# Earlier load requests, and a last weight chunk in two column halves, in an attention and soft-MoE kernel

## The chip, the cores and the metric

The kernel runs on one core of one Trainium2 chip. The metric is the device time in microseconds of one execution, the median of several runs. The profile is one profiled execution on the chip, with a time of its own. Engines: PE is the matrix engine TensorE (PEld is its weight load), DVE is VectorE, ACT is ScalarE, POOL is GpSimd and SP is SyncE, which here only issues transfers. Each engine works through its own program in order. Transfers run on 16 DMA engines that all queues share.

## What is computed

The reference is attention with 16 extra "beacon" keys and values ahead of the sequence, and a soft mixture of experts on its output:

```python
# q, k, v: (8 batches, 8 heads, 576, 64); beacon_k, beacon_v: (8, 8, 16, 64), float32
k_all, v_all = concat([beacon_k, k], 2), concat([beacon_v, v], 2)
scores = q @ k_all^T / 8                # causal over the 576, the beacons always seen
x = softmax(scores) @ v_all             # as 4608 tokens x 512
# phi: (512, 32 slots), w1: (8 experts, 512, 1024), w2: (8, 1024, 512)
logits = x @ phi
d = softmax(logits, axis=0)             # over the tokens
slot_input = (d.T @ x).reshape(8, 4, 512)
slot_out[e] = relu(slot_input[e] @ w1[e]) @ w2[e]
out = softmax(logits, axis=1) @ slot_out
```

No output row can be formed before the last expert's weights have been used, since each output token mixes all 32 slots.

## The kernel before

**The order of the work.** The order on every engine is the order of the program's text; there is no scheduler that moves work. Buffers come from pools that rotate: a load into a buffer waits until the last reader of its earlier content is done, and it is issued at its place in the program of its engine, so whatever stands behind it on that engine waits too.

**Attention** runs over 32 pairs of heads, n = 0 to 31; batch b = n // 4, and g = n % 4 is the pair within the batch. Iteration n (L758 to L797) issues the scores of pair n (`scores`, four banks; ScalarE takes the exponential, L526, and GpSimd masks it, `select`, L512), the transposes of the keys (even n) or queries (odd n) of the next half batch (`transposes`, L490), and the product of pair n-1's masked scores with the values (`attend`, L542). So `attend(4)` stands in iteration 5. At g = 1, 2 and 3 the values of the next batch are cast (`cast_v`, L391 and L395), and at g = 3 they are permuted (`perm_v`). In `perm_v` GpSimd copies the 16 beacon values into place (L410), in order with its masks. Iterations 0 and 1 are written out ahead of the loop, with all loads that fit at the start.

**Loads.** k and q come by half batches (a half batch is four heads, numbered m = 2b + hb here) through four buffers each; v and its remainder `vrem` by batches through two buffers each; the beacon values `bvst` through one buffer. All of them are issued by SyncE (only the first q by ScalarE). At g = 0 of batch b SyncE's program has the beacon values of batch b + 1, then v of b + 2, then k and q of its first half; at g = 2 the remainder of v and the second half.

**Weights.** The 16.8 MB of expert weights, as float16, come in 32 chunks of 512 KB (`wchunks`). GpSimd issues them, since they are cast on the way from float32. `load_weights(count)` at the end of an iteration issues the next `count` of them. Experts 0 to 4 have memory of their own (expert 4 among them with both matrices); expert 5 uses the two v buffers (`wv`), experts 6 and 7 the k and q buffers (`wt`), once attention is done with them. The last chunk, `WLAST`, is half of the second matrix of expert 7; it comes as two transfers, each of two of its four row groups c.

**The end.** `first` and `second` are the two expert matrices, for four experts at a time in the four column groups of TensorE. `second(eg, c0, c1, halves)` adds the row groups c0 to c1 into the left (256 columns) and right accumulators. The left half is scaled into `so1` by VectorE (L873), the right by ScalarE (L876). Then every token's output is one matmul with `so1` (L924), scaled on the way out of PSUM by VectorE (L931) or ScalarE (L929) in turn, and stored three token columns j at a time (L935), 768 KB each; the first three columns are stored as one and two.

```python
        second(1, 0, NFC - 2)
        second(1, NFC - 2, NFC, (0,))
        nc.vector.tensor_scalar(out=so1[:, 0:HW], in0=so[0], scalar1=rd[:, 0:1], scalar2=None,
                                op0=AL.mult)
        second(1, NFC - 2, NFC, (1,))
        nc.scalar.activation(so1[:, HW:Dm], so[1], AF.Copy, scale=rd[:, 0:1])
```

Behind it stands a test of value ranges (`judge`) and a general path that is entered only if the test fails.

Of the kernel before, what the change touches and what calls it, by code (L numbers as in the profile page):

```python
# [9 lines left out]
FP = mybir.dt.float32  # L10
# [3 lines left out]
AL = mybir.AluOpType  # L14
AF = mybir.ActivationFunctionType
# [36 lines left out]
NJ = 9  # L52
# [216 lines left out]
def kernel(  # L269
# [12 lines left out]
    nc = tc.nc  # L282
    P = 128
    B, H, S, D = q.shape
    Nb = beacon_k.shape[2]
    E, Dm, F = moe_w1.shape
# [3 lines left out]
    NFC = F // P  # L290
# [4 lines left out]
    scale = 1.0 / (D ** 0.5)  # L295
# [45 lines left out]
        g = n % NG  # L341
        return 2 * g + hh if n >= NPAIR - 2 else 4 * (g // 2) + 2 * hh + g % 2

    def load_qk(b, hb, first=False):
        for src, tag in ((k, "k"), (q, "q")):
            t = st[tag, b, hb] = stq.tile([P, 2, NJ, D], FP, name=f"{tag}stag", tag=tag)
            sr = src[b].rearrange("h (p j) d -> (h p) (j d)", j=NJ)
            eng = nc.scalar if first and tag == "q" else nc.sync
            for h0, h1 in ((0, 1), (1, 2)) if first else ((0, 2),):
                lo = 256 * hb + P * h0  # L350
                eng.dma_start(
                    out=t[:, h0:h1, :, :].rearrange("p h j d -> p h (j d)"),
                    in_=sr[lo:lo + P * (h1 - h0), :].rearrange("(h p) e -> p h e", p=P))

    def load_v(b):

        t = st["v", b] = stv.tile([P, H, 4, D], FP, name="vstag", tag="v", bufs=2)
        st["r", b] = stv.tile([P, H, D], FP, name="vrem", tag="r", bufs=2)
        h0 = 0 if b else 1
        lo = ((b * H + h0) * S - Nb) * D
        nc.sync.dma_start(
            out=t[:, h0:H, :, :].rearrange("p h t d -> p h (t d)"),
            in_=v.rearrange("b h s d -> (b h s d)")[lo:lo + (H - h0) * S * D].rearrange(
                "(h e) -> h e", h=H - h0)[:, 0:4 * P * D].rearrange("h (p e) -> p h e", p=P))
        if b == 0:
            nc.vector.memset(t[0:4, 0, :, :], 0.0)  # L370
            for p0, p1 in ((4, 116), (116, 128)):
                nc.sync.dma_start(
                    out=t[p0:p1, 0, :, :].rearrange("p t d -> p (t d)"),
                    in_=v[b, 0, 4 * p0 - Nb:4 * p1 - Nb, :].rearrange("(p t) d -> p (t d)", t=4))

    def load_vr(b):
        nc.sync.dma_start(out=st["r", b][0:80, :, :],
                          in_=v[b, :, 496:576, :].rearrange("h p d -> p h d"))

    def load_bv(b):  # L380

        st["bv", b] = stv.tile([Nb, H, D], FP, name="bvst", tag="bv", bufs=1)
        nc.sync.dma_start(out=st["bv", b][:, :, :], in_=beacon_v[b].rearrange("h n d -> n h d"))
# [39 lines left out]
    def piece(e, m, j):  # L423

        if e < NRES:
            if m == 0:
                return w1h[e][:, 2 * j:2 * j + 2, :].rearrange("p t f -> p (t f)")
            return w2h[e][:, 4 * j:4 * j + 4, :].rearrange("p c d -> p (c d)")
        if (e, m, j) not in wtail:
            if e == NRES:  # L430
                t = stv.tile([P, 2, 2048], F16, name="wv", tag="v", bufs=2)
                for i in range(2):
                    wtail[e, m, i] = t[:, i, :]
            else:
# [10 lines left out]
    def load_weights(count):  # L445
        for _ in range(count):
            if not wchunks:
                return
            e, m, j = wchunks.pop(0)
            if m == 0:  # L450
                nc.gpsimd.dma_start(
                    out=piece(e, m, j),
                    in_=moe_w1[e, 2 * j * P:2 * (j + 1) * P, :].rearrange("(p t) f -> p (t f)", t=2))
            else:
                src = moe_w2[e].rearrange("(p c) d -> p c d", c=NFC)
                cs = 2 if (e, m, j) == WLAST else 4
                for c in range(0, 4, cs):
                    nc.gpsimd.dma_start(
                        out=piece(e, m, j)[:, c * Dm:(c + cs) * Dm],
                        in_=src[:, 4 * j + c:4 * j + c + cs, :].rearrange("p c d -> p (c d)"))  # L460

    qTs = {}

# [213 lines left out]
    with tc.manual_schedule(engines={ET.PE, ET.DVE, ET.Activation, ET.Pool, ET.SP}):  # L677
# [11 lines left out]
        load_vr(1)  # L689
        phif = acc[:, 0:NDC * NSL].rearrange("p (c e) -> p c e", c=NDC)  # L690
        nc.sync.dma_start(out=phif, in_=moe_phi.rearrange("(c p) e -> p c e", p=P))
        load_bv(1)

        nc.gpsimd.memset(eT[:, 0:512], 1.0)
        nc.gpsimd.memset(onesh[:, :], 1.0)  # L695
# [57 lines left out]
        transposes(1, 1)  # L753
        scores(1, 3)
        load_v(2)
        load_qk(2, 0)

        for n in range(2, NPAIR):  # L758
            b, g = divmod(n, NG)
            scores(n, 0)  # L760
            scores(n, 1)
            if n == 2:
                cast_v(1, 0)
            if n // 2 + 1 < 2 * B:
# [12 lines left out]
            if b and g == 2:  # L777
                logits(b - 1)
            if n >= 8 and g == 0:
                dispatch(b - 2)  # L780
            if b + 1 < B and g:
                if b or g > 1:
                    cast_v(b + 1, g - 1)
                if g == 3:
                    perm_v(b + 1)
            if b + 1 < B and g == 0:
                load_bv(b + 1)
            if b + 2 < B:
                if g == 0:
                    load_v(b + 2)  # L790
                    load_qk(b + 2, 0)
                if g == 2:
                    load_vr(b + 2)
                    load_qk(b + 2, 1)
            if n == 5:
                nc.vector.tensor_copy(out=phih[:, :, :], in_=phif)
            load_weights(0 if b == 0 else (0, 1, 1, 1)[g] if b < 6 else (1, 2, 2, 2)[g] if b == 6 else 2)  # L797
        siz = work.tile([P, NDC, E * (NSL + SPE)], F16, name="siz", tag="qT")
        nc.gpsimd.memset(siz[:, :, :], 0.0)
        load_weights(len(wchunks))  # L800
# [79 lines left out]
        ps_f = fast.enter_context(tc.tile_pool(name="ps_f", bufs=6, space=PSUM))  # L880
        outr = out.rearrange("(a p j) d -> a p j d", p=P, j=NJ)


        gd = fast.enter_context(tc.tile_pool(name="gdp", bufs=1))
# [29 lines left out]
        JS = [(0, 3), (3, 6), (6, 9)]  # L914
        cnt = 0
        for bb in range(4):
            for (j0, j1) in JS if bb else [(0, 1), (1, 3)] + JS[1:]:
                osb = m3.tile([P, 3, Dm], FP, name="osb", tag="osb")
                for j in range(j0, j1):
                    hw = Dm // 2 if cnt == 0 else Dm  # L920
                    fp_ = [ps_f.tile([P, Dm], FP, name="fps", tag="fps")
                           for _ in range(Dm // hw)]
                    for i, f in enumerate(fp_):
                        nc.tensor.matmul(f[:, 0:hw], row_tokens(bb, j),  # L924
                                         so1[:, hw * i:hw * i + hw], start=True, stop=True)
                    for i, f in enumerate(fp_):
                        ou = osb[:, j - j0, hw * i:hw * i + hw]
                        if (cnt + i) % 2:
                            nc.scalar.activation(ou, f[:, 0:hw], AF.Copy, scale=rc[:, bb, j:j + 1])  # L929
                        else:  # L930
                            nc.vector.tensor_scalar(out=ou, in0=f[:, 0:hw],  # L931
                                                    scalar1=rc[:, bb, j:j + 1], scalar2=None,
                                                    op0=AL.mult)
# [41 lines left out]
```

## Time and profile before

| what | value |
|---|---|
| median of 3 runs | 201.09 us (200.14 to 202.2) |
| the profiled execution | 200.37 us |
| its span, first to last instruction | 198.7 us |
| PE busy | 160.2 us (81%) |
| DVE, ACT, POOL busy | 135.1, 133.9, 118.6 us |
| read from memory, written to it | 62.71 MB, 9.44 MB |
| loads of SyncE and stores | 25,736 packets, 38.01 MB, 53.4% of 16 engines' span |
| weights (GpSimd's queue) | 4,752 packets, 16.78 MB, 43.2% |

A line of a timeline gives the start in us from the span's start, the length, the engine, the program line, the operation, what it writes and reads, and how many were merged; in brackets stands the idle time of the engine before it and what ended it. In a table by stretch, each engine's busy time is followed by its number of instructions; then come the granted TensorE clock (1.00 is full), the mean busy share of the DMA engines, and GB/s. The bytes of the weights are counted as they arrive (float16), so that weights alone read some 213 GB/s with all engines full. The DMA share can pass 1, because the packets of one DMA engine overlap a little. The records behind the page also hold the landings of each transfer (one on each of the DMA engines that take part) and the start, length and size of each packet.

### The profile page before, as it was taken

The numbers are of one execution on the slowest core, as the hardware profiler recorded it, in microseconds if no ns is written. First come the engines' busy times: TensorE is split into PE (matmuls) and PEld (weight loads), VectorE is DVE, ScalarE is ACT, GpSimd is POOL, SyncE is SP. The second block draws the span as 40 slices with busy tenths as digits, with TensorE's granted clock in tenths as the row PEclk, the third lists the DMA queues.
The fourth block names the chain that finished last, engine by engine and source line by source line (L and its number), as shares of the span: only waits on it lengthen the run. The fifth ranks groups of instructions, "written<-read, shape, count | busy, mean of one in ns | idle before, by whom it ended". The sixth has DMA issues, their size and how long they took to land.

```text
span 198.7 us, 7454 instructions
## 1 busy us (share of the span) xinstructions
PE 160.2 (81%) x3160; PEld 107.9 (54%) x3160; DVE 135.1 (68%) x282; ACT 133.9 (67%) x173; POOL 118.6 (60%) x270
## 2 busy tenths in 40 slices
PE   6978697898998989889898998988899944984400
PEld 2525455675774867567586576756676622541000
DVE  1497778888878887878898888888373300797400
ACT  3285678888887898888888889888942200892400
POOL 6074396697596678759758877997873000781000
PEclk9999999999999999999999999999999995897555
DMA  6999998999999999999999999999999994399992
GB/s 214 352 380 406 355 365 261 366 332 179 237 386 277 235 373 315 258 305 366 259 255 366 290 273 199 188 178 215 214 210 214 212 213 91 153 426 428 416 417 80
DMA packets 30817, 55.93 MB, mean 282 GB/s; under 512 B 8380, under 2 KB 16568, under 8 KB 30776
## 3 DMA queue, kind: packets, MB, share of 16 engines
q1 hardware_dynamic: 25736, 38.01, 53.4%
q0 software_dynamic: 4752, 16.78, 43.2%
q8 instruction: 26, 0.43, 0.8%
q10 hardware_dynamic: 288, 0.59, 0.8%
q14 instruction: 15, 0.12, 0.2%
HBM read 62.71 MB, written 9.44 MB: 363 GB/s over the span
## 4 chain that ended last, share of the span: by engine, by line
PE 55%; DMA 16%; ACT 8%; DVE 7%; POOL 5%; issue 3%; ACTq 0%; DVEq 0%; POOLq 0%
DMA wt<-in_moe_w_dram 14%; PE av L542 13%; PE sc L521 13%; PE trps L490 8%; PE fps L924 5%; PE xtps L568 5%; ACT vh L408 4%; ACT expT L526 3%; PE vpt L405 2%; POOL expT L512 2%; PE vps L405 2%; DMA bkf<-in_beacon_k_dram 2%; PE lgps L587 2%; PE sips L626 2%; DVE sel L729 2%
## 5 line engine op out<-in xcount | busy, mean ns | idle before, releaser
L526 ACT ACTIVATE expT<-sc 128x992 f16<-128x992 f32 (+3 forms) x128 | 104.3, 868 | 17.6 <-PE sc L521 16.8
L512 POOL TENSOR_SCALAR_AFFINE_SELECT expT<-expT 128x224 f16<-128x224 f16 (+3 forms) x128 | 55.2, 442 | 28.2 <-ACT expT L526 27.0
L521 PE MATMUL sc<-qT,kT 64*128 64x80 bf16 (+4 forms) x576 | 43.0, 244 | 12.1 <-ACT expT L526 5.7
L542 PE MATMUL av<-vh,expT 128*128 128x65 f16 (+1 forms) x960 | 40.3, 194 | 0.4 <-issue 0.2
L542 PEld LDWEIGHTS <-expT 128*128 128x128 f16 (+1 forms) x960 | 33.5, 98 | 4.1 <-issue 1.0
L521 PEld LDWEIGHTS <-kT 64*128 64x128 bf16 x576 | 17.1, 95 | 28.6 <-issue 21.4
L502 DVE COPY kT<-trps 128x640 bf16<-128x640 bf16 (+1 forms) x31 | 22.7, 773 | 8.9 <-PE trps L490 8.4
L502 DVE COPY qT<-trps 128x640 bf16<-128x640 bf16 (+1 forms) x31 | 22.7, 772 | 8.0 <-PE trps L490 6.9
L556 DVE TENSOR_TENSOR x<-av,r 128x640 f16<-128x640 f32 x32 | 26.4, 824 | 1.1
L391 POOL CAST vc<-vstag 128x512 f16<-128x512 f32 x30 | 17.5, 613 | 3.3 <-PE sc L521 3.3
L575 DVE COPY xT<-xtps 128x576 f16<-128x576 f16 x31 | 14.2, 457 | 4.3 <-PE xtps L568 4.3
L929 ACT ACTIVATE osb<-fps,rc 128x512 f32<-128x512 f32 (+1 forms) x19 | 11.9, 675 | 5.0 <-PE fps L924 4.5
L931 DVE TENSOR_SCALAR osb<-fps,rc 128x512 f32<-128x512 f32 (+1 forms) x18 | 12.2, 724 | 2.5 <-PE fps L924 2.3
L568 PE MATMUL xtps<-idh,x 128*128 128x128 f16 (+2 forms) x160 | 13.7, 216 | 0.1
L924 PE MATMUL fps<-so,eT 128*128 128x512 f16 (+1 forms) x37 | 12.0, 456 | 0.4 <-ACT osb L929 0.2
L893 POOL TENSOR_SCALAR lo<-so 128x512 f32<-128x512 f16 x1 | 1.5, 1508 | 17.8 <-ACT so L876 17.8
L568 PEld LDWEIGHTS <-x 128*128 128x128 f16 (+2 forms) x160 | 8.9, 97 | 5.1 <-issue 4.7
L490 PE MATMUL trps<-idb,kstag 128*64 128x128 bf16 x270 | 10.6, 222 | 0.6 <-DVE vh L412 0.5
L412 DVE CAST vh<-vpt 128x512 f16<-128x512 f32 x16 | 10.3, 683 | 1.2 <-PE vpt L405 1.2
L490 PE MATMUL trps<-idb,qstag 128*64 128x128 bf16 x270 | 10.5, 222 | 0.2 <-DVE kT L502 0.2
L662 PE MATMUL fill<-eT,onesh 128*128 128x512 f16 x26 | 9.2, 473 | 1.7 <-POOL onesh L695 1.5
L408 ACT ACTIVATE vh<-vps 128x1024 f16<-128x1024 f32 x8 | 8.2, 1026 | 3.4 <-PE vpt L405 3.4
(102 smaller groups left out, 205.1 us busy)
## 6 DMA issues: line engine op xcount, KB each, us to landing
kstag<-in_k_dram SPq DMA_DIRECT2D x15, 576.0 KB, 11.1
qstag<-in_q_dram SPq DMA_DIRECT2D x15, 576.0 KB, 12.2
out_dram<-osb SPq DMA_DIRECT2D x11, 768.0 KB, 7.2
vstag<-in_v_dram SPq DMA_DIRECT2D x7, 1024.0 KB, 9.4
w1h<-in_moe_w_dram POOLq DMA_DIRECT2D x10, 512.0 KB, 8.2
w2h<-in_moe_w_dram POOLq DMA_DIRECT2D x10, 512.0 KB, 8.0
wt<-in_moe_w_dram POOLq DMA_DIRECT2D x7, 512.0 KB, 13.4
wv<-in_moe_w_dram POOLq DMA_DIRECT2D x4, 512.0 KB, 11.7
```

The costliest lines, as they stand in the source:

```text
L391: (nc.vector if c == 1 and b == 0 else nc.gpsimd).tensor_copy(out=st["c", b][:, :, hs, :].rearrange("p t h d -> p h t d"), in_=st["v", b][ ...
L408: nc.scalar.activation(vhs[b % 2][:, 0:2, :, 0:D], ps[:, :, :].rearrange("p c (h d) -> p c h d", d=D), AF.Copy)
L490: nc.tensor.transpose(tp[lo:hi, j - j0, :], t[:, hh, j, :].bitcast(BF)[:, 1::2], idb[:, :])
L502: nc.vector.tensor_copy(out=do, in_=ti)
L512: nc.gpsimd.affine_select(out=ap, in_=ap, compare_op=AL.is_ge, fill=0.0, base=cbase, pattern=pat, channel_multiplier=-1)
L521: nc.tensor.matmul(sc[:, hh, col:col + qw], kTs[n // 2 % 2][po:po + D, n % 2, c * P:(c + 1) * P], qTs[n // 2][po:po + D, n % 2, q0:q0 + qw ...
L526: nc.scalar.activation(ex[:, :, base:base + w], sc[:, :, 0:w], AF.Exp, scale=scale)
L542: nc.tensor.matmul(av[:, i, :], exps[n % 2][0:KW[c], hh, o:o + P], vhs[b % 2][0:KW[c], c, h, :], start=(c == 0), stop=(c == i))
L556: nc.vector.tensor_tensor(out=xs[b][:, :, head(n, 0):head(n, 1) + 1:head(n, 1) - head(n, 0), :].rearrange("p i h d -> p h i d"), in0=av[:, ...
L568: nc.tensor.transpose(tp[:, QLO[i]:QLO[i] + QW[i]], xs[b][0:QW[i], i, 2 * t:2 * t + 2, :].rearrange("p h d -> p (h d)"), idh[0:QW[i], 0:QW ...
L575: nc.vector.tensor_copy(out=xT[:, t, 0:S], in_=tp[:, :])
L924: nc.tensor.matmul(f[:, 0:hw], row_tokens(bb, j), so1[:, hw * i:hw * i + hw], start=True, stop=True)
```

## The change

Three things change; what is computed stays the same.

1. **Requests for loads.** k and q of half batch m + 4 are asked for in the iteration whose transposes free their buffer (k at even n, q at odd n); v of batch b + 3 at g = 2 of batch b, after the cast that frees its buffer; its remainder and the beacon values of b + 2 at g = 3. Ahead of the loop, k and q of half batch 4 move to the place where the beacon values of batch 1 stood, and these come last, behind v of batch 2, half batch 5 and the remainder of v. Weights start in batch 0 (one chunk each in iterations 2 and 3), and iteration 25 issues one chunk where it issued two.
2. **The last chunk** comes as its left and its right 256 columns, all four row groups in each, in runs of 512 bytes on arrival.
3. **The end.** `second` does row groups 4 to 7 for the left half, then the left halves of token columns 0 to 5 of the first 1,152 tokens are computed, scaled (the first three by one VectorE product, the next three by ScalarE copies), put where the masked scores were, and stored as two transfers of 384 KB. Then follow row groups 4 to 7 of the right half, and the right halves of these six columns as two stores of 384 KB. All other columns are stored as before, in threes.

```diff
-    def load_qk(b, hb, first=False):
+    def load_qk(b, hb, first=False, tags="kq"):
         for src, tag in ((k, "k"), (q, "q")):
+            if tag not in tags:
+                continue
...
-                src = moe_w2[e].rearrange("(p c) d -> p c d", c=NFC)
-                cs = 2 if (e, m, j) == WLAST else 4
-                for c in range(0, 4, cs):
-                    nc.gpsimd.dma_start(
-                        out=piece(e, m, j)[:, c * Dm:(c + cs) * Dm],
-                        in_=src[:, 4 * j + c:4 * j + c + cs, :].rearrange("p c d -> p (c d)"))
+                src = moe_w2[e].rearrange("(p c) d -> p c d", c=NFC)[:, 4 * j:4 * j + 4, :]
+                dst = piece(e, m, j).rearrange("p (c d) -> p c d", c=4)
+                if (e, m, j) != WLAST:
+                    nc.gpsimd.dma_start(out=dst.rearrange("p c d -> p (c d)"),
+                                        in_=src.rearrange("p c d -> p (c d)"))
+                    continue
+                for c0 in (0, Dm // 2):
+                    nc.gpsimd.dma_start(out=dst[:, :, c0:c0 + Dm // 2],
+                                        in_=src[:, :, c0:c0 + Dm // 2])
...
-        load_bv(1)
+        load_qk(2, 0)
...
         scores(1, 3)
         load_v(2)
-        load_qk(2, 0)
+        load_qk(2, 1)
+        load_vr(2)
+        load_bv(1)
...
-            if b + 1 < B and g == 0:
-                load_bv(b + 1)
-            if b + 2 < B:
-                if g == 0:
-                    load_v(b + 2)
-                    load_qk(b + 2, 0)
-                if g == 2:
-                    load_vr(b + 2)
-                    load_qk(b + 2, 1)
+            if b + 3 < B and g == 2:
+                load_v(b + 3)
+            if n // 2 + 5 < 2 * B:
+                load_qk(*divmod(n // 2 + 5, 2), tags="kq"[n % 2])
+            if g == 3:
+                if b + 2 < B:
+                    load_bv(b + 2)
+                if b + 3 < B:
+                    load_vr(b + 3)
...
-            load_weights(0 if b == 0 else (0, 1, 1, 1)[g] if b < 6 else (1, 2, 2, 2)[g] if b == 6 else 2)
+            load_weights((0, 1, 1, 1)[g] if b < 6 else (1, 1, 2, 2)[g] if b == 6 else 2)
...
-        second(1, 0, NFC - 2)
-        second(1, NFC - 2, NFC, (0,))
+        second(1, 0, NFC // 2)
+        second(1, NFC // 2, NFC, (0,))
         nc.vector.tensor_scalar(out=so1[:, 0:HW], in0=so[0], scalar1=rd[:, 0:1], scalar2=None,
                                 op0=AL.mult)
-        second(1, NFC - 2, NFC, (1,))
+        for i in range(2):
+            fl = ps_sc.tile([P, 4, HW], FP, name="fls", tag="sc")
+            ol = exps[i][:, :, :].rearrange("p a x -> p (a x)").bitcast(FP)[
+                :, 0:3 * HW].rearrange("p (j d) -> p j d", j=3)
+            for j in range(3):
+                nc.tensor.matmul(fl[:, j, :], row_tokens(0, 3 * i + j), so1[:, 0:HW], start=True,
+                                 stop=True)
+            if i == 0:
+                nc.vector.tensor_tensor(
+                    out=ol, in0=fl[:, 0:3, :],
+                    in1=rc[:, 0, 0:3].unsqueeze(2).broadcast_to([P, 3, HW]), op=AL.mult)
+            else:
+                for j in range(3):
+                    nc.scalar.activation(ol[:, j, :], fl[:, j, :], AF.Copy,
+                                         scale=rc[:, 0, 3 + j:4 + j])
+            nc.sync.dma_start(out=outr[0, :, 3 * i:3 * i + 3, 0:HW], in_=ol)
+        second(1, NFC // 2, NFC, (1,))
         nc.scalar.activation(so1[:, HW:Dm], so[1], AF.Copy, scale=rd[:, 0:1])
...
-            for (j0, j1) in JS if bb else [(0, 1), (1, 3)] + JS[1:]:
+            for (j0, j1) in JS:
                 osb = m3.tile([P, 3, Dm], FP, name="osb", tag="osb")
+                lo_ = HW if bb == 0 and j0 < 6 else 0
...
-                nc.sync.dma_start(out=outr[bb, :, j0:j1, :], in_=osb[:, 0:j1 - j0, :])
+                nc.sync.dma_start(out=outr[bb, :, j0:j1, lo_:Dm], in_=osb[:, 0:j1 - j0, lo_:Dm])
```

More of the change, by code (lines that the diff above doesn't have):

```diff
@@ L870 @@
         second(0, NFC // 2)
-        second(1, 0, NFC - 2)
-        second(1, NFC - 2, NFC, (0,))
+        second(1, 0, NFC // 2)
+        second(1, NFC // 2, NFC, (0,))
         nc.vector.tensor_scalar(out=so1[:, 0:HW], in0=so[0], scalar1=rd[:, 0:1], scalar2=None,
                                 op0=AL.mult)
-        second(1, NFC - 2, NFC, (1,))
+        outr = out.rearrange("(a p j) d -> a p j d", p=P, j=NJ)
+        for i in range(2):
[15 more added lines that the diff above has]
+        second(1, NFC // 2, NFC, (1,))
         nc.scalar.activation(so1[:, HW:Dm], so[1], AF.Copy, scale=rd[:, 0:1])
@@ L880 @@
         ps_f = fast.enter_context(tc.tile_pool(name="ps_f", bufs=6, space=PSUM))
-        outr = out.rearrange("(a p j) d -> a p j d", p=P, j=NJ)
         gd = fast.enter_context(tc.tile_pool(name="gdp", bufs=1))
@@ L916 @@
         for bb in range(4):
-            for (j0, j1) in JS if bb else [(0, 1), (1, 3)] + JS[1:]:
+            for (j0, j1) in JS:
                 osb = m3.tile([P, 3, Dm], FP, name="osb", tag="osb")
+                lo_ = HW if bb == 0 and j0 < 6 else 0
                 for j in range(j0, j1):
[L920 to L933, printed above, removed]
+                    f = ps_f.tile([P, Dm], FP, name="fps", tag="fps")
+                    nc.tensor.matmul(f[:, lo_:Dm], row_tokens(bb, j), so1[:, lo_:Dm], start=True,
+                                     stop=True)
+                    ou = osb[:, j - j0, lo_:Dm]
+                    if cnt % 2:
+                        nc.scalar.activation(ou, f[:, lo_:Dm], AF.Copy, scale=rc[:, bb, j:j + 1])
+                    else:
+                        nc.vector.tensor_scalar(out=ou, in0=f[:, lo_:Dm],
+                                                scalar1=rc[:, bb, j:j + 1], scalar2=None,
+                                                op0=AL.mult)
                     cnt += 1
-                nc.sync.dma_start(out=outr[bb, :, j0:j1, :], in_=osb[:, 0:j1 - j0, :])
+                nc.sync.dma_start(out=outr[bb, :, j0:j1, lo_:Dm], in_=osb[:, 0:j1 - j0, lo_:Dm])
                 if bb in (0, 1) and j0 == 3:
```

## The prediction

> **What bounds the kernel now.** I read the page's 40 slices first, then busy time by stretch, then the timelines of GpSimd, SyncE and TensorE, and last the records of each load's landing and each DMA packet.
>
> ```profile
> PEclk9999999999999999999999999999999995897555
> DMA  6999998999999999999999999999999994399992
> ```
>
> Slices are 4.97 us. The DMA engines are full from slice 1 to slice 32 (to 164 us), nearly empty in slices 33 and 34, and full again to slice 38. TensorE, the busiest engine, has nothing left to do from about 161 us but wait for the last weights. So two things set the end: when the last load lands, and how fast the stores start after it. Stretches of 5 us (columns: PE, PEld, DVE, ACT, POOL busy, granted clock, DMA share, GB/s) show where the DMA engines were not full:
>
> ```profile
> 30.00:35.00 5.00, 3.79 (x85) 2.76 (x86) 3.95 (x8) 4.46 (x6) 3.06 (x8) 1.00 0.87 261
> ...
> 45.00:50.00 5.00, 4.39 (x89) 2.66 (x85) 4.50 (x9) 4.19 (x5) 3.79 (x9) 1.00 0.93 167
> 50.00:55.00 5.00, 4.49 (x108) 3.36 (x110) 4.44 (x11) 4.21 (x7) 2.52 (x6) 1.00 0.97 259
> ...
> 120.00:125.00 5.00, 4.49 (x107) 3.41 (x104) 4.29 (x10) 4.34 (x6) 3.99 (x10) 1.00 0.98 183
> 125.00:130.00 5.00, 5.00 (x112) 3.45 (x111) 4.03 (x9) 4.43 (x6) 4.87 (x12) 1.00 1.00 201
> 130.00:135.00 5.00, 4.39 (x121) 3.26 (x117) 4.44 (x9) 4.24 (x5) 4.50 (x11) 1.00 1.02 176
> ...
> 165.00:170.00 5.00, 3.25 (x31) 1.71 (x31) 0.70 (x2) 0.47 (x1) 0.23 (x1) 0.50 0.25 46
> 170.00:175.00 5.00, 5.00 (x35) 3.21 (x34) 4.25 (x9) 4.73 (x8) 4.92 (x5) 0.92 0.63 256
> ```
>
> Full stretches read 1.06, since packets overlap a little. In the six stretches before 135 us the shortfall is 0.59 x 5 / 1.06 = 2.8 us of DMA time; in the last two it is about 5.8 us.
>
> **Part 1, loads earlier: what it can gain.** If all six gaps closed, the last load would land 2.8 us earlier. It lands at 168.1 us on the slowest of the 16 DMA engines, but at 166.4 on the median one; the slow one has work while the others idle, so for it I count some 1.5 us. Bounds -2.8 to 0.
>
> **What it moves behind.** SyncE issues the beacon values of batch 1 (32 KB, L383) at 17.36 now, ahead of v of batch 2 and four k/q loads. In the new order they come behind all of those. GpSimd needs them here (timeline: start, length, engine, line):
>
> ```profile
> 30.63 0.61 POOL L410 CAST vh<-bvst 16x512 f16<-16x512 f32 x1 [0.34 <-ACT vh L408]
> 31.52 0.38 POOL L512 TENSOR_SCALAR_AFFINE_SELECT expT<-expT 128x224 f16<-128x224 f16 x1 [0.29 <-ACT expT L526]
> ```
>
> When would they land? Loads of SyncE finish in order, and from 5 to 30 us the DMA engines are full. The last of the loads that would now be ahead is this q, issued at 25.06 and landed 9.9 us later, at 34.9:
>
> ```profile
> 25.06 1.26 SPq L351 DMA_DIRECT2D qstag<-in_q_dram  x1
> ```
>
> ```profile
> qstag<-in_q_dram SPq DMA_DIRECT2D x1, 576.0 KB, 9.9
> ```
>
> The same bytes through full engines cannot land sooner. Besides, a first weight chunk now goes out at the end of iteration 2, about 28.0 us, right after the second cast of v (ends 28.02). A chunk alone takes 2.46 us (spacing of the last landings), and between 77 and 80 us, with both queues backlogged, the weight queue held 75% of the engines against 33%, so all 2.46 us would come ahead of the beacon values: 34.9 + 2.5 = 37.4. Bounds 34.9 and 37.4; I take the later one, since the chunk is issued 7 us before. GpSimd runs in order. Queued behind its wait are a weight issue (0.55 us), the four masks of pair 4 (0.38, 0.41, 0.64, 0.33) and the beacon-key copies (0.52): 37.4 + 0.6 + 0.55 + 2.3 = 40.9. TensorE takes pair 4's masked scores from 35.32 to 35.95 today (the attend on line L542 of iteration 5); it would end near 41.1. **Compute slips 5.2 us** (2.7 at the lower bound). With TensorE busy 4.2 to 5.0 of each 5 us until 145, the slip is not made up.
>
> **What the slip costs.** TensorE itself has cover: it has been waiting for weights since 159.3, with the last at 168.1. The weight issues are the trouble, since they stand in GpSimd's program:
>
> ```profile
> 118.59 0.55 POOL L458 DMA_DIRECT2D w2h<-in_moe_w_dram  x1
> 123.46 1.08 POOL L451 DMA_DIRECT2D w1h<-in_moe_w_dram  x2
> 127.81 1.08 POOL L458 DMA_DIRECT2D w2h<-in_moe_w_dram  x2
> ```
>
> By then all other loads are through, and the weights alone must keep the engines full. Counting on the median engine: 16 chunks and all other loads are done at 124.2 today, with 1.9 us of gaps behind them, so at 122.3 without. The change has one chunk more in this work by then (two in batch 0, one fewer in iteration 25): 124.8. Chunk 18 is issued at 118.6 + 5.2 and starts 1.9 us later (the delay from 123.46 to its first data): 125.7, done 128.2. Chunk 19: 123.5 + 5.2 + 1.9 = 130.6, done 133.1. Chunks 20 and 21: 127.8 + 5.2 + 1.9 = 134.9, done 139.8, and landed 0.3 later, 140.1. Today chunk 21 lands at 138.9. After that the queue never runs dry in either kernel. So three new gaps (0.9, 2.4, 1.8) take the place of the closed ones: the last load is +1.2 on the median engine. The slow engine, some 1.7 us behind, sees about 1.4 us less of the gaps: -0.2. I take **+0.6**.
>
> **Part 2, left and right columns.** The last chunk's 256 packets of 2,048 bytes (173 ns each) become 1,024 of 512 bytes. Packets of 4,096 bytes took 324 ns, so 150 ns per 2,048 and 22 fixed: 60 ns for 512, and a half takes 512 x 60 / 16 = 1.9 us where it took 1.4. Two halves: at most +0.9, at least 0 if the fixed part overlaps; I take **+0.4**. [...]
>
> **Part 3, left halves stored in between.** Added: six matmuls of 256 columns, one VectorE product of 768 elements, three ScalarE copies of 256 (0.474 each, L929), two stores of 384 KB. Removed: the same columns later. Their cover is the wait for the right columns (1.2 us between landings today). Left lands at T; four rounds of L849 (0.1 us apart at full clock, 0.2 at half) and the scaling (0.48) give T + 1.0; the first matmuls, +0.35; the product, 0.24 + 768 x 0.00094 = 0.96 (from 0.48 for 256 and 0.72 for 512 elements); first data 0.86 after the issue (170.64 to 171.50): T + 3.2. Right lands at T + 1.6, but its scaling waits on ScalarE for the three copies, until T + 3.3, and its first store has data near T + 5.5. The two early stores take 2.0 us, so 0.3 us stay empty. Today's stores start at T + 4.6 (166.9 to 171.5) and run 23.2 us. Half-width packets of 1,024 bytes add: 82 ns for 2,048 and 159 for 4,096 give 43 ns, 1,536 x 43 / 16 = 4.1 against 256 x 234 / 16 = 3.7: +0.4. Together, with T itself counted above: -1.4 + 0.3 + 0.4 = **-0.7**. If TensorE is at half clock here as today (0.50), 0.4 to 1.0 of it goes: bounds -1.9 (both stores wholly hidden) and +0.4.
>
> **Sum.** +0.6 + 0.4 - 0.7 = +0.3. The profiled execution took 200.37 us, 198.7 of span and 1.7 around it; the change would make it 200.7. The median of the runs stands 0.7 above that execution: 201.09 + 0.3 = **201.4**.
>
> **Rivals.** *The gaps close and nothing slips.* For it: TensorE may still have work past 35 us, or the beacon values may overtake. Then -1.5 to -2.8 for the loads, +0.4 for the packets, -0.3 for the tail at half clock: about -2.2, 198.9. Against it: loads landed in order throughout.
>
> *The slip grows, and the kernel is slower.* TensorE would stand idle from about 35.4 to 39.1. An idle time of 1.94 us (from 19.6) left the clock at 1.00; one of 3.5 us before 181.7 stands in a stretch with 0.61. If the clock falls to half, the following 3.5 us of matmuls take some 1.7 us more. Later beacon values also sit behind more loads than today: those of batch 6 would follow a q that landed at 118.5 now, and are wanted at 114.5 + 5.2. The point from which it decides is a slip of about 7 us: chunks 18 to 20 each start that much later, and each further us costs nearly one at the end. A slip of 8 gives 201.4 + 2.7 = 204.1. [...]
>
> *Nothing changes*, because engines that are full already gain nothing from earlier requests: 201.1.
>
> **Chances.** About 1% (2 us) is what a measurement of this kernel can tell from no change. The forecast 0.45 (own range 199.8 to 203.0), the faster rival 0.27, the slower 0.25, nothing 0.03. Faster by over 1% holds four fifths of the first rival: 0.22. Slower: three quarters of the second and an edge of the forecast: 0.25. The rest, 0.53, within 1%. As both signs hold half the chance, the range takes both: 198.6 to 204.1.
>
> **What would show it.** L410 of batch 1 starting near 37 instead of 30.6; TensorE idle 35 to 39; a DMA share below 1.0 again between 123 and 136; the last weights near 168.5; first store data about 1.4 us sooner behind the left columns. I am wrong if the beacon values land before 32, if the DMA share holds 1.06 up to 164, or if the slip passes 7 us.

## The result and the profile after

The changed kernel took **204.22 us** (median of six runs, 203.15 to 205.37); the kernel before took 201.69 (six runs, 200.14 to 203.55). The ratio is **1.0139 [1.0092, 1.0186]**: slower by 1.4%. The profiled execution took 203.36 us, 201.6 of it span. Here and below an interval compares undisturbed runs only, and where that leaves some out, the medians of all runs stand beside it.

The first view is the 40 slices of the page, of the changed kernel (a slice is 5.04 us, a digit is tenths):

```profile
PEclk9999999757999999999999999999999999787555
DMA  6999999996799999999999999969999999499992
```

Two things are new here. TensorE's granted clock falls in slices 7 to 9 (35 to 50 us), and the DMA engines, which were full in slices 9 and 10 and around 131 us, are not. Next the timeline of GpSimd at 36 us (start, length, engine, line; in brackets the idle time before it and what ended it):

```profile
35.94 0.61 POOL L412 CAST vh<-bvst 16x512 f16<-16x512 f32 x1 [5.01 <-DMA bvst<-in_beacon_v_dram]
36.50 0.56 POOL L453 DMA_DIRECT2D w1h<-in_moe_w_dram  x1
37.07 0.75 POOL L517 TENSOR_SCALAR_AFFINE_SELECT expT<-expT 128x224 f16<-128x224 f16 x2
```

The copy of batch 1's beacon values stood at 30.63 before; it now waits 5.01 us for its transfer. That transfer was issued at 24.96 and landed on the median DMA engine at 31.94, but on the last at 35.83, and the copy needs all. The masks of pair 4 start at 37.07. TensorE's timeline shows who waits for them:

```profile
37.52 0.70 PE L547 MATMUL av<-vh,expT 128*128 128x65 f16 x5 [2.16 <-POOL expT L517]
39.05 0.73 PE L547 MATMUL av<-vh,expT 128*128 128x65 f16 x10 [0.83 <-POOL expT L517]
```

In the kernel before, the same product of pair 4 ran without a wait:

```profile
35.32 0.63 PE L542 MATMUL av<-vh,expT 128*128 128x65 f16 x15
```

TensorE is done with pair 4 at 39.8 instead of 35.95, so 3.8 us late. But the loss goes on. The stretches of 5 us (PE, PEld, DVE, ACT, POOL busy, granted clock, DMA share, GB/s):

```profile
35.00:40.00 5.00, 1.89 (x33) 1.20 (x27) 1.45 (x2) 1.03 (x2) 3.90 (x10) 0.77 1.06 370
40.00:45.00 5.00, 4.55 (x66) 3.30 (x63) 2.64 (x7) 3.24 (x4) 2.73 (x6) 0.50 1.07 301
45.00:50.00 5.00, 5.00 (x100) 3.88 (x97) 2.88 (x6) 2.98 (x5) 3.11 (x9) 0.71 0.76 175
50.00:55.00 5.00, 4.39 (x85) 2.58 (x81) 4.24 (x10) 4.34 (x7) 3.85 (x9) 1.00 0.71 160
...
125.00:130.00 5.00, 4.49 (x110) 3.32 (x106) 4.45 (x10) 4.21 (x7) 3.06 (x7) 1.00 0.95 179
130.00:135.00 5.00, 5.00 (x128) 3.93 (x124) 3.71 (x8) 4.47 (x7) 4.86 (x12) 1.00 0.74 120
135.00:140.00 5.00, 4.39 (x100) 2.63 (x96) 4.20 (x10) 4.34 (x7) 4.38 (x10) 1.00 0.90 153
```

The kernel before, from 40 to 45 us:

```profile
40.00:45.00 5.00, 5.00 (x124) 4.00 (x124) 4.06 (x9) 4.54 (x6) 4.82 (x13) 1.00 1.07 322
```

There TensorE did 124 matmuls in 5.00 us; in the changed kernel it is busy for 4.55 us with 66, so at a clock of 0.50 one takes some 1.7 times as long. Compared at the same iteration, a weight issue comes 4.8 us later than before in iteration 5, 6.7 in iteration 9 and 7.8 in iteration 23.

The late issues leave the DMA engines empty in two places. From 45 to 52.5 us they idle for 3.0 us (the idle time of the 16 engines in sum, divided by 16). SyncE's timeline shows why:

```profile
38.03 2.09 SPq L353 DMA_DIRECT2D qstag<-in_q_dram  x1
50.08 0.37 SPq L367 DMA_DIRECT2D vstag<-in_v_dram  x1
```

The load of v of batch 4 goes into the buffer that GpSimd's late casts set free; SyncE stands at it from 40 to 50 us, until the last of these casts ends at 50.05, with k, q, beacon values and remainder queued behind it. From 122.5 to 137.5 the engines idle for 2.8 us more: all other loads are through, and GpSimd's weight issues come too late. From 5 to 160 us the engines idle for 6.1 us in all, before for 2.4. That is the difference at the end: the last weights land at 170.71 us on the median engine and 171.58 on the last, where they landed at 166.45 and 168.12. Behind that landing the end is a little shorter than before (28.07 us to the last store's landing instead of 28.46). So +3.5 - 0.4 = 3.1 us stand beside the 3.0 us by which the two profiled executions differ.

### The profile page after: what moved, and what is told of

Same layout as the page of the kernel before. It is cut to its first block, busy times and chain, and to the rows that moved or that the text cites. A ratio compares the mean times of both kernels' runs of the same rounds, so it can differ in the third digit from the quotient of the medians.

```text
span 201.6 us, 7472 instructions
## 1 busy us (share of the span) xinstructions
PE 163.3 (81%) x3165; PEld 110.6 (55%) x3165; DVE 136.0 (67%) x283; ACT 134.1 (67%) x175; POOL 119.3 (59%) x270
## 5 line engine op out<-in xcount | busy, mean ns | idle before, releaser
L526 PE MATMUL sc<-qT,kT 64*128 64x80 bf16 (+4 forms) x576 | 43.9, 249 | 12.1 <-ACT expT L531 5.7
L547 PE MATMUL av<-vh,expT 128*128 128x65 f16 (+1 forms) x960 | 42.6, 197 | 4.3 <-POOL expT L517 3.2
L547 PEld LDWEIGHTS <-expT 128*128 128x128 f16 (+1 forms) x960 | 35.1, 100 | 8.7 <-POOL expT L517 3.8
L953 ACT ACTIVATE osb<-fps,rc 128x512 f32<-128x512 f32 (+1 forms) x18 | 10.8, 651 | 5.8 <-PE fps L949 5.1
L573 PE MATMUL xtps<-idh,x 128*128 128x128 f16 (+2 forms) x160 | 14.2, 221 | 0.1
L495 PE MATMUL trps<-idb,kstag 128*64 128x128 bf16 x270 | 11.1, 228 | 0.6 <-DVE vh L414 0.5
L495 PEld LDWEIGHTS <-kstag 128*64 128x64 bf16 x270 | 8.6, 114 | 4.4 <-issue 4.2
L412 POOL CAST vh<-bvst 16x512 f16<-16x512 f32 x8 | 4.9, 608 | 9.6 <-DMA bvst<-in_beacon_v_dram 5.0
```

The costliest lines, as they stand in the source:

```text
L495: nc.tensor.transpose(tp[lo:hi, j - j0, :], t[:, hh, j, :].bitcast(BF)[:, 1::2], idb[:, :])
L526: nc.tensor.matmul(sc[:, hh, col:col + qw], kTs[n // 2 % 2][po:po + D, n % 2, c * P:(c + 1) * P], qTs[n // 2][po:po + D, n % 2, q0:q0 + qw ...
L547: nc.tensor.matmul(av[:, i, :], exps[n % 2][0:KW[c], hh, o:o + P], vhs[b % 2][0:KW[c], c, h, :], start=(c == 0), stop=(c == i))
L573: nc.tensor.transpose(tp[:, QLO[i]:QLO[i] + QW[i]], xs[b][0:QW[i], i, 2 * t:2 * t + 2, :].rearrange("p h d -> p (h d)"), idh[0:QW[i], 0:QW ...
```

## The experiments

Each ratio compares runs with runs of the kernel before on the same chip. Line numbers are the changed kernel's unless it is said otherwise.

The theory: the late beacon values of batch 1 stall GpSimd, TensorE stalls and loses its clock, and all later requests slip. Against it stood that the loads' new order or the thinner weight schedule opens the gaps by itself (A), and that the new end is the cost (B).

**Batch 1's beacon values back at their place.**

```diff
+        load_bv(1)
         load_qk(2, 0)
...
         load_vr(2)
-        load_bv(1)
```

> The changed kernel, but the beacon values of batch 1 are asked for at their old place, ahead of k and q of half batch 4. Theory (the late beacon values stall GpSimd, the stall and the slower clock behind it put every later request back by 7 us): the copy of the beacon values starts near 30.6 again, TensorE has no stall at 35 to 39, the weight issues of the late iterations come at the times of before or sooner, the last weights land 1 to 3 us sooner than in the kernel before on the median DMA engine, and the time is 2 to 3 us below before (ratio 0.985 to 0.990). Rival A (the order of the loads and the thinner weight schedule of iteration 25 open the gaps by themselves): gaps of 2 us or more stay between 45 and 55 and between 120 and 137, and the time is at or above before (ratio 1.00 to 1.01). Rival B (the end is the cost): the time stays at 1.01 although the loads are early.

Ratio **0.9934 [0.9888, 0.998]** (medians 200.65 and 201.06): 2.0% of the time goes with this one line. The copy starts at 32.36 without a wait for its load, the engines idle for 0.1 us between 5 and 120. B falls. But the gain is about half of what was expected. In the profiled execution the last weights land no sooner than before (at 166.58 us on the median engine and 168.47 on the last), where 1 to 3 us were expected, and 2.1 us of idle time stay between 122.5 and 137.5, as rival A said for that place. GpSimd's timeline shows a reason further on:

```profile
83.60 0.61 POOL L412 CAST vh<-bvst 16x512 f16<-16x512 f32 x1 [1.17 <-DMA bvst<-in_beacon_v_dram]
...
103.16 0.61 POOL L412 CAST vh<-bvst 16x512 f16<-16x512 f32 x1 [3.69 <-DMA bvst<-in_beacon_v_dram]
```

With the first stall gone, the beacon values of two later batches (4 and 5) are late. In the changed kernel the compute was already 7 us behind by then, and these waits did not show.

**The same delay in the kernel before.** It moves that one transfer alone (there the later half batch 5 comes in iteration 2):

```diff
-        load_bv(1)
...
                     load_qk(b + 2, 1)
+                    if b == 0:
+                        load_bv(1)
```

> The kernel before, with one transfer moved: the beacon values of batch 1 (32 KB) are asked for behind v of batch 2, half batches 4 and 5 and the remainder of v, in iteration 2; no weights are asked for early. Theory: the beacon values land 2 to 5 us later than GpSimd wants them, GpSimd and TensorE stall, and this alone makes the kernel 1.5 to 4 us slower than before (ratio 1.008 to 1.02). Rival A (only the new order of all loads together with the weight schedule costs the time): the stall is there but is made up before the end, ratio 0.997 to 1.003. Rival C (without the early weight chunks there is no stall at all, since the beacon values land by 31): ratio 1.00 and no idle time at the copy.

Ratio 1.0038 [0.9998, 1.0078] (medians 202.26 and 201.06): little, between the theory and its rivals. GpSimd waits 3.58 us (copy at 33.74), but no weight issue stands behind the copy, and TensorE is done with pair 4 at 36.8, only 0.9 us later than before, at a clock of 1.00. So GpSimd's masks had some 2 us to spare, and a stall of 3.6 us lies almost wholly within them; one of 5 us with an issue behind it does not.

**The end by itself**, first the old end in the changed kernel, then the new end (last chunk in columns, left halves in between) in the kernel before; the edits are the change's own lines.

> The changed kernel with the end of before: the last chunk in row groups and no left halves in between. Theory (the end is worth a little, the loss is all in the loads): 0.4 to 1 us slower than the changed kernel, so a ratio to before of 1.017 to 1.020. Rival B (the column halves and the early stores are the cost): 1.0 to 1.005.

> The kernel before with only the new end: the last chunk as left and right columns, six left halves stored in between. Theory: 0.2 us more for the packets and 0.4 to 1.2 us less behind them, a ratio of 0.995 to 1.000. Rival B: a ratio of 1.005 to 1.015.

Ratios 1.0167 [1.011, 1.0224] (medians 204.72 and 201.06) and 1.0016 [0.9979, 1.0053] (201.85 and 201.06). The second alone bounds the end's cost at -0.4 to +1.1 us. Neither tells it from nothing, and B does not explain the 1.4%: with the old end the loss stays.

**The clock by itself.** Nine matmuls whose result is not used, ahead of the product of pair 4, keep TensorE busy in its stall:

```diff
+            if n == 5:
+                fill(9)
             attend(n - 1, 0)
```

> The changed kernel with nine extra matmuls of 512 columns (1.9 us at full clock, their result is not used) ahead of the product of pair 4, in iteration 5, where TensorE stands still while GpSimd waits for the beacon values. Theory: the stall of GpSimd stays at 5 us, but the granted clock holds 1.00 between 35 and 50, the slip of everything behind is 5.3 us instead of 7.2, and 1 to 2 us of the loss go: ratio to before 1.004 to 1.009. Rival D (the slower clock costs nothing that the stall has not cost already): ratio 1.014 as without the fill.

Ratio **1.0019 [0.9976, 1.0061]** (medians 202.37 and 201.30): 2.4 us less than the changed kernel by the ratios, 1.5 by the medians, where 1 to 2 were expected, although GpSimd's copy starts no sooner (wait of 5.49 us, copy at 35.95). The stretches of this run:

```profile
35.00:40.00 5.00, 3.38 (x33) 1.79 (x33) 1.18 (x2) 0.64 (x2) 3.88 (x10) 1.00 1.07 380
40.00:45.00 5.00, 4.43 (x114) 3.46 (x112) 4.23 (x11) 4.21 (x6) 3.73 (x9) 1.00 1.07 300
45.00:50.00 5.00, 5.00 (x105) 3.21 (x102) 4.07 (x8) 4.35 (x7) 4.35 (x10) 1.00 0.96 239
```

The clock holds at 1.00; the slip is 3.6 us instead of 6.7 in iteration 9 and 5.2 instead of 7.8 in iteration 23, and the gap after 45 us nearly closes (0.4 us of idle time up to 52.5 instead of 3.0). So 2.6 to 3.1 us of the slip were the clock, and they made most of the loss. Rival D falls.

**The first weight chunk an iteration later**, behind the copy of the beacon values:

```diff
-            load_weights((0, 1, 1, 1)[g] if b < 6 ...
+            load_weights((0, 0, 0, 2)[g] if b == 0 else (0, 1, 1, 1)[g] if b < 6 ...
```

> The changed kernel with the first weight chunk asked for in iteration 3 together with the second, behind GpSimd's copy of the beacon values, instead of in iteration 2. Theory: this chunk lay ahead of the beacon values on the DMA engines; without it they land some 2.4 us sooner, the stall of GpSimd falls from 5.0 us to 2.5 to 3, TensorE is idle for less than 1 us and keeps its clock, the slip is some 3 us instead of 7.2, and the time is 1.000 to 1.006 of before. Rival E (the beacon values are late only because of the loads of SyncE's own queue): the stall stays at 4 to 5 us and the ratio at 1.01 to 1.015.

Ratio 1.0225 [1.0172, 1.0278], a clear miss. The beacon values did land sooner (34.07 on the last engine, 1.8 us), so the chunk had been ahead of them there. GpSimd came to the copy 1.1 us sooner too, so its wait stayed at 4.71 us, as rival E had it for another reason. And something else came in. GpSimd's timeline:

```profile
34.55 0.61 POOL L412 CAST vh<-bvst 16x512 f16<-16x512 f32 x1 [4.71 <-DMA bvst<-in_beacon_v_dram]
39.41 0.79 POOL L453 DMA_DIRECT2D w1h<-in_moe_w_dram  x1 [4.26 <-issue]
```

Behind the copy GpSimd pauses for 4.26 us, for nothing that the profile shows ("issue"), then the masks are late and TensorE is idle for 6.28 us. Among the records, one packet of 8 KB of the queue that carries instructions was moved at 37.48. Was GpSimd waiting for the next part of its own program? Eight tiny memsets at the start of its program, in idle time, shift the place at which that would happen:

```diff
         nc.gpsimd.memset(xT[:, :, S:S + 48], 0.0)
+        for _ in range(8):
+            nc.gpsimd.memset(xT[:, 0, S:S + 2], 0.0)
```

> The run with the first chunk in iteration 3 (its GpSimd paused 4.3 us between the copy of the beacon values and the first weight issue, for nothing that the profile shows, while one 8 KB packet of instructions was moved at 37.5), with eight tiny memsets more at the start of GpSimd's program, in its idle time at 4 to 6.6 us. Theory F: GpSimd waited there for the next block of its own program, which came late through full DMA engines; eight instructions earlier the border of the block falls ahead of the wait for the beacon values, the fetch is hidden in it, the first weight issue follows the copy at once, TensorE's stall falls from 6.3 us to about 2, and the ratio from 1.022 to 1.000 to 1.010. Rival G: the pause belongs to the first weight issue itself when the engines are full; it stays at about 4 us and the ratio at 1.018 to 1.026.

Ratio 0.9997 [0.9955, 1.004] (median 201.48 against 201.15). The same place in this run:

```profile
33.95 0.61 POOL L412 CAST vh<-bvst 16x512 f16<-16x512 f32 x1 [1.77 <-DMA bvst<-in_beacon_v_dram]
34.51 1.34 POOL L453 DMA_DIRECT2D w1h<-in_moe_w_dram  x2
```

The pause is gone, and 5 us (medians 206.50 and 201.48) with it, by adding instructions. So the weight issue alone does not make the pause, and rival G falls; one trace with it and one without point to the place in the program. That it is the loading of the program fits the packet, but no record names whose it was, so this stays open. In this execution TensorE had also lost its clock from 22.8 to 29.7 us (0.78 and 0.53 in the stretches 20 to 25 and 25 to 30), which would have hidden part of the wait.

**One chunk more in iteration 24**, first with the late beacon values kept, then with batch 1 put back:

```diff
-            load_weights(... (1, 1, 2, 2)[g] if b == 6 else 2)
+            load_weights(... (2, 1, 2, 2)[g] if b == 6 else 2)
```

> The changed kernel with the late beacon values kept, but two chunks instead of one asked for in iteration 24, so that one chunk more is queued from there on. Theory: of the 6 us in which the DMA engines idle, the 2.8 us between 120 and 137 are a queue of weights that runs dry, and one chunk (2.5 us) more in it closes most of them; the 3 us between 45 and 53 stay. Ratio 1.000 to 1.006. Rival A in its weak form (the engines' gaps late in the kernel are not what delays the end): ratio 1.012 or more.

> The beacon values of batch 1 at their old place and two chunks asked for in iteration 24. Theory: no gap of more than 0.5 us in all between 5 and 165 us, the last weights 1.5 to 2.5 us sooner than with the beacon values at their old place alone, ratio to before 0.980 to 0.988. Rival A: as without the extra chunk, 0.990 to 0.996.

The first has a median of 201.43 against 201.3, with runs from 196.54 to 204.81 and no interval; in its profiled execution the clock had fallen at 15 to 20 us (0.72 in that stretch), the compute was late by itself, and of the stall 1.28 us were left. The second has **0.9863 [0.9811, 0.9915]**: 0.7% below batch 1 alone, with intervals that overlap. The traces are clearer: the engines' idle time from 120 to 160 us goes from 2.3 to 0.9 us, and the last weights land 2.3 us sooner (164.24 on the median engine). The thin weight schedule is thus a cost of its own, the weaker half of A.

**A fill in TensorE's wait at 19.6 to 21.5**, on top:

```diff
         scores(1, 3)
+        fill(6, False)
```

> The best kernel so far (beacon values at their old place, two chunks in iteration 24) with six matmuls of 512 columns (1.3 us, result not used) in the 1.94 us for which TensorE waits at 19.6 to 21.5 for the queries' transposes. In five of the ten profiled executions so far the granted clock fell below 0.85 in the stretch 20 to 25 behind this wait, in the others not. Theory: with the fill the clock stays at 1.00 from 15 to 35, the copy of the beacon values starts at 29.8 to 30.8, and the time is 0.980 to 0.986 of before, with less spread. Rival: the clock falls all the same, or the 1.7 us that it costs there is hidden, and the ratio stays at 0.986 to 0.990.

Ratio 0.9806 [0.9727, 0.9885], but the median of all six is 199.26 against 201.15 (0.991), and the runs scatter from 196.28 to 203.45: not told from the run without the fill. The clock was 1.00 in all stretches read from 15 to 55 and from 75 to 85 us, as expected up to 35. Then came this:

```profile
79.96 0.61 POOL L397 CAST vh<-vrem 80x512 f16<-80x512 f32 x1
85.22 0.61 POOL L412 CAST vh<-bvst 16x512 f16<-16x512 f32 x1 [4.66 <-DMA bvst<-in_beacon_v_dram]
```

Again beacon values, those of batch 4. This is the third trace in which a later batch's are late as soon as the compute keeps its time. They are asked for only when their single buffer is free, one batch ahead.

**All beacon values a batch sooner.** The remainder of v leaves 48 of 128 partitions empty, and it has two buffers; the beacon values fit in there:

```diff
-        st["bv", b] = stv.tile([Nb, H, D], FP, name="bvst", tag="bv", bufs=1)
-        nc.sync.dma_start(out=st["bv", b][:, :, :], ...)
+        nc.sync.dma_start(out=st["r", b][96:96 + Nb, :, :], ...)
...
+        load_bv(1)
         load_qk(2, 0)
...
         load_vr(2)
-        load_bv(1)
+        load_bv(2)
...
-                if b + 2 < B:
-                    load_bv(b + 2)
                 if b + 3 < B:
                     load_vr(b + 3)
+                    load_bv(b + 3)
```

> The changed kernel with the beacon values of every batch a batch sooner: they come into 16 partitions that the remainder of v leaves free in its two buffers, the first three ahead of the loop, the others together with that remainder, two batches ahead of their use. Weights as in the changed kernel. Theory (with the first stall gone, the beacon values of batch 4, 5 or 6 became the next late ones: GpSimd waited 3.7 to 4.7 us for them with only batch 1 put back): no wait of GpSimd for beacon values over 0.5 us in any batch, every request of the late iterations 2 to 4 us sooner, ratio to before 0.980 to 0.988. Rival A: the late stalls were hidden behind the full DMA engines, and the ratio stays at 0.990 to 0.997 as with batch 1 alone.

> The same with two chunks in iteration 24. Theory: 0.976 to 0.984, no gap of the DMA engines between 5 and 164 us over 0.3 us. Rival: the DMA engines are full in both, so the same as without the extra chunk (0.980 to 0.988), or 0.986 as with batch 1 alone.

> The same with six matmuls (result not used) in TensorE's wait at 19.6 to 21.5. Theory: the clock holds at 1.00 up to 50 us, and since the DMA engines are full either way, the time is as without the fill to 0.5%: 0.974 to 0.984. Rival: each of the first 50 us that TensorE loses still counts at the end; then it is 0.005 or more below the run without the fill.

Ratios **0.9725 [0.9655, 0.9794]** (medians 197.73 and 201.91), **0.9699 [0.9649, 0.9749]** (195.24) and **0.9675 [0.9632, 0.9718]** (194.99), each below the range expected for it. GpSimd waits for no beacon values in any batch. In the first of the three, the copy for batch 4, which had waited 4.66 us above, follows half a us behind the copy of the remainder (the lines are 411 and 396 here):

```profile
79.81 0.61 POOL L396 CAST vh<-vrem 80x512 f16<-80x512 f32 x1
80.97 0.61 POOL L411 CAST vh<-vrem 16x512 f16<-16x512 f32 x1 [0.55 <-POOL vh L396]
```

Beside the changed kernel's 1.0139, the place of these 32 KB transfers, one a batch, is worth some 4%, twice what putting batch 1 back showed. Rival A of this run falls. The slices of the second, with the extra chunk, show engines that stay full:

```profile
PEclk9999889999999999999999999999999799996555
DMA  6999999999999999999999999999999995699992
```

They idle for 0.2 us from 5 to 160, and the last weights land at 161.46 on the median engine, 5.0 us sooner than before. Only 2.3 of these 5.0 are idle time saved. The time of the load and weight packets, summed over 16 engines, is nearly the same in both kernels (168.9 and 168 us), so most of the rest would be packets that overlap more; this stays open. The clock lost at 20 to 25 us in this run (the 8s; 0.73 in that stretch) cost nothing that the fill brings back by more than the intervals.

All three beat both kernels, the two with the extra chunk the kernel before by 3%; those two are not told apart.

## Why the prediction was wrong

**The first half of the chain held.** The beacon values were put at 37.4, between 34.9 and 37.4; they landed at 35.83 and the copy started at 35.94. The masks, the weight issue ahead of them and TensorE's wait followed as worked out, 1.3 us sooner (pair 4 done at 39.8 instead of 41.1). The lower bound holds for the slowest engines alone: fourteen of the 16 had delivered by 32.7 us, before the "same bytes" of the q load at 34.9.

**The slip, "Compute slips 5.2 us", is the step that failed.** The stall alone made 3.6 us, and 5.2 by iteration 23 (the run with nine matmuls), so the figure was right for a kernel that keeps its clock. The clock made it 6.7 and 7.8. The forecast put the clock at nothing; it was in the text, but in a rival, and with a condition: TensorE idle from 35.4 to 39.1 in one piece. It was idle for 2.16 us, busy for 0.70 and idle for 0.83, and the clock still fell to 0.50. The rival also let it fall for 3.5 us, at a cost of 1.7. That length was the author's estimate: in the kernel before, the fall behind 164 us lasted 6.83 us. In the changed kernel the clock stayed at half for 10.24 us, and the slip grew by 3.1.

Whether the clock falls varies from execution to execution. After the same 1.94 us of idling at 19.6, which the prediction counted as harmless from one execution, it fell below 0.90 (to 0.67 to 0.84 in the stretch 20 to 25) in 7 of the 13 profiled executions of kernels without a fill there.

The records of the granted clock show what set these 7 apart. In the traces of the two kernels every record of the clock but the last is a whole multiple of 3.41 us long (30.72, 10.24, 126.29, 3.41 and 6.83 us in the changed kernel; 157.01, 6.83 and 10.24 before), so there the changes lie on a grid. In the 7 the clock was low behind the wait for 3.4 or 6.8 us, from 21.7 us on in one execution and from 24.0 in another, so the grid lies elsewhere in each. In the six of them whose TensorE timeline was read there, the wait of 1.94 us lay whole within one step of the grid, with TensorE busy for 1.47 or 1.48 us of the step, and the clock fell at the end of that step. In three of the other 6 (both kernels, and the run with the first chunk an iteration later) a border of the grid cut the wait in two, the longer part 1.02 to 1.44 us, and the clock held; for the last three the place of the grid is not shown. That the prediction saw it hold was the luck of one execution. The stall of the changed kernel, from 35.36 to 37.52, lay within the step from 34.26 to 37.67, and the clock fell at 37.67. In the nine traces whose steps can be read from 18 to 45 us, the clock fell from 1.00 after steps in which TensorE was busy for 0.80 to 1.48 us, and after none with 1.98 or more. In the run with all beacon values sooner and the extra chunk it also fell between 149.9 and 154.7 us (the 7 in its slices); what set that off is not shown.

**For a kernel that keeps its clock the sum came near, but not by its terms.** It gave 201.4 beside 201.09, a ratio of 1.0015; the run with the stall but without the loss of clock has 1.0019 [0.9976, 1.0061]. In that run's profiled execution, though, the last weights land 1.8 us later than before on the median engine and on the last (168.29 and 169.87), not 0.6. So the agreement is in part luck.

**"What the slip costs", +0.6, measured +4.3 us on the median engine and +3.5 on the last.** Three new gaps of 5.1 us in sum were expected between 122 and 137; there were 2.8, at that place. What was missed is the other 3.0 us at 45 to 52.5. The text followed GpSimd's weight issues alone and named the weights "the trouble", but SyncE's loads wait for buffers that the same late engines set free. The late beacon values of other batches were named in the rival, for batch 6; they came for batches 4 and 5, and only where the first stall was gone.

**The columns of the last chunk, +0.4, measured +0.2:** the halves landed 1.33 us apart on the last engine and 1.37 on the median, where the two halves of before took 1.22 and 1.28; that is 0.1 for one half, and 0.2 if both cost the same. The packets of 512 bytes did take 60 ns, as worked out, which makes 1.9 us for a half; the landings stand closer than that, so packets overlap. (By the prediction's own figures its upper bound is +1.1, not +0.9.)

**The left halves in between, -0.7, are not settled.** First store data came 3.8 us behind the left columns on the last engine, not 3.2, and 2.4 behind the right columns where the kernel before took 3.4. From the last landing to the last store's landing the time changed by -1.2 us on the median engine and -0.4 on the last, at a clock of 0.92 in the stretch 170 to 175 in both. The new end as a whole, by itself, is 0.3 us [-0.4, +1.1] dearer, where -0.3 was predicted.

**The rivals.** "The slip grows, and the kernel is slower" is what happened, with nearly its time (204.1 for a slip of 8; measured 204.22 with 7.8). That the times meet is in part luck: the rival looked for each us beyond 7 in the gaps behind iteration 23. There the idle time grew only from 2.1 us (slip of 5.2, the run with nine matmuls) to 2.8 (7.8), while from 45 to 52.5 it grew from 0.4 to 3.0. Its point of decision is not shown. "The gaps close and nothing slips" is what batch 1 put back does, in part (0.9934 for its 0.989).

## What to carry to other kernels

Order loads by when the last DMA engine delivers against when the first reader wants them, not by size: a 32 KB transfer asked for last cost more here (2.0% with batch 1 alone) than the earlier requests brought with it back in its place (0.7%). When a stall is found, price it with the clock that may fall behind it, and ask what waits for buffers on every issuing queue, not only the one in view. After a stall is taken away, look for the next reader of the same kind: a late kernel hides it.

## What was not expected of the hardware

- The landings of one small transfer spread widely, at a DMA share of 1.11 (30 to 35 us): batch 1's beacon values had landed on the median engine at 31.94 us and on the last at 35.83, so 3.9 us of the stall were the wait for a few engines: the last two landings came at 35.8, the one before them at 32.7.
- 1.94 us of idling halved TensorE's clock for the next 3.4 to 6.8 us, or not, from one execution to the next, by where the wait lay on a grid of 3.41 us in the nine traces that show both; 2.16 us in the changed kernel halved it for 10.24. The kernel's runs scatter by about 1% either way; that this comes from the clock is not shown. With six to nine matmuls in the idle time the clock was 1.00 there in all three kernels that had them.
- In one trace GpSimd paused for 4.26 us between two of its instructions for nothing in the profile; in the trace with eight instructions more ahead of that place the pause was gone.
